# Windowed attention and a feed-forward layer: converting w_in further ahead, and giving a softmax's sums and divisions to GpSimd

## The chip, the cores and the metric

The kernel runs on one core of a Trainium2 chip, the other cores being unused. The metric is the device time of one execution in microseconds (us), the median of several runs. Engines are named as the profile names them: PE is TensorE (matmuls), DVE is VectorE, ACT is ScalarE, POOL is GpSimd, SP is SyncE, which here only issues transfers. PE and PEld are the two rows of TensorE, matmuls and weight loads.

## The reference

Eight heads of causal attention with a window of 128 positions and a linear bias, over 8 sequences of 576 positions, then a feed-forward layer (FFN) with a smooth rectifier:

```python
scores = scale * np.matmul(q, k.transpose(0, 1, 3, 2))          # q, k, v: (8, 8, 576, 64) float32
bias = slopes[:, None, None] * (-np.abs(rel).astype(np.float32))[None, :, :]
mask = (rel >= 0) & (rel < window)                              # window = 128
attn = softmax(np.where(mask, scores + bias[None], -1000000000.0))
x = np.matmul(attn, v)                                          # as (4608, 512)
h = x @ w_in                                                    # w_in: (512, 2048) float64
g = np.where(h >= 1, h, np.where(h <= -1, 0.0, (h + 1) ** 2 / 4))
return (g @ w_out).astype(np.float32)                           # w_out: (2048, 512) float64
```

The weights arrive in 64-bit floating point. The kernel has to turn them into 32-bit numbers itself, and it splits most of its operands into a high and a low 16-bit half, so that three 16-bit matmuls stand for one of higher precision.

## The kernel before, in words

**Tiling.** The 4608 rows are worked off in 12 chunks of 384 rows (three tiles of 128). For each chunk the attention of 8 heads is done as 4 pairs of heads, p = 4c to 4c + 3 for chunk c, and then the FFN over 16 blocks fc of 128 of the 2048 inner columns. While PE does the FFN of chunk c, the attention of chunk c + 1 is worked off between its blocks.

**Attention.** `scores` (L433) multiplies q and k of a pair. `soften` (L465) adds the bias and finds the maximum on DVE (L482, writes `z` and `nmax`), takes the exponential and its sum on ACT (L484), then on DVE sums up (L490), takes the reciprocal (L491), adds the two halves of z, which belong to neighbouring key blocks (L494), and multiplies by the reciprocal into `ep` (L495). `weights_t` (L499) transposes `ep` on PE (L504), copies on ACT (L508) and cuts out the two triangles on POOL (L509, L511) into `lu`. `values` (L525) multiplies by v on PE (L538), and `split_x` (L576) makes the 16-bit halves of x (L583, L584). `reach_of` and `reach_of_v` (L308, L380) take the largest value of v's rows on DVE (L385), for a common scale of x. `done_t[m]` marks the end of head m's `weights_t`.

**FFN.** `layer1` (L587) does 12 matmuls per block (L590 to L592) and the rectifier: `u` on ACT (L597), `g` in two steps on DVE (L598, L599). `done_g[fc]` marks the rectifier's instructions. `layer2` (L610) follows two blocks later; in chunk 0 it multiplies 32-bit numbers (L619), later 16-bit halves (L622 to L624), for which `g` is split by ACT and POOL (L606, L607).

**Weights.** In chunk 0's FFN the weights of each block are also brought in and converted. `fetch_weights(fc)` (L171) loads a block's w_in and w_out, 512 KB each, into one of three buffers `raw`, by two DMAs on ACT's queue (L173, L175). `convert_in` (L189) unfolds the two words on ACT (L180, L181), joins them on DVE (L185) and takes the largest value of each row (L194). `convert_out` (L216) joins w_out's words (L185) and scans them on ACT (L219). `scale_in` (L197) spreads the largest values over the partitions with a small PE matmul (`across`, L152, writes `m_i`) and works out the scale on DVE (L159 to L163). `split_in` (L204) makes the halves `wi` on ACT (L210) and DVE (L211). The first three blocks are converted during chunk 0's attention, each half of the work behind the head that `EARLY` (L761) names; `then` (L773) puts the scales and splits of blocks 0 and 1 and chunk 0's row reductions behind heads. In the FFN `convert_after(f)` (L749) converts block f + 3 and scales block f + 2 behind the rectifier of block f, and block f + 2 is split at the end of it.

**Order.** The program text gives each instruction a rank. A planner simulates the engines with costs of its own before the kernel is built and puts onto each engine, and into each DMA queue, the instruction of the best rank that is ready in its simulation. On the chip each engine and each queue then works strictly in that order. `behind(instructions, f)` (L238) forces what f issues behind the given instructions on the same engine. The attention's steps are a list, `segments` (L655 to L712), emitted as far as a count (`emit_attention`, L713); `ready[c]` marks the place in it from which chunk c's FFN can begin, and the loop at L799 emits a share of the next chunk's segments after each half block. Of pair 4, which is chunk 1's first, the scores stand ahead of the last values of chunk 0, so they come before chunk 0's FFN. `keep_busy` (L85) fills PE with transposes that nobody reads during chunk 0's attention.

Of the kernel before, what the change touches and what calls it, by code (L numbers as in the profile page):

```python
# [20 lines left out]
def windowed_attention_then_ffn(  # L21
# [26 lines left out]
    P = 128  # L48
# [92 lines left out]
    def column(name, tag, bufs=2, n=1):  # L141
        return ap1.tile([P, n], F32, name=name, tag=tag, bufs=bufs)
# [28 lines left out]
    def fetch_weights(fc):  # L171
        w = raw[fc] = rawp.tile([P, 2, DM, 2], I32, name=f"raw{fc}", tag=f"raw{fc % 3}")
        S.dma_start(w[:, 0].rearrange("p (c f) w -> p c f w", c=NCC),  # L173
                    wi32[:, 2 * fc * P:2 * (fc + 1) * P].rearrange("(c p) (f w) -> p c f w", p=P, w=2))
        S.dma_start(w[:, 1], wo32[fc * P:(fc + 1) * P, :].rearrange("p (f w) -> p f w", w=2))  # L175
# [11 lines left out]
    wide = {}  # L187

    def convert_in(fc):  # L189
        f = wide[fc] = wp.tile([P, DM], F32, name=f"f_i{fc}", tag="f_i", bufs=3)  # L190
        unfold(fc)
        float32_of(fc, 0, f)
        rows = column(f"rows_i{fc}", "rows")
        V.tensor_reduce(rows, f, X, ALU.max, apply_absolute_value=True)  # L194
        spread(f"i{fc}", rows)

    def scale_in(fc):  # L197
        s1, i1 = s_in[:, fc:fc + 1], i_in[:, fc:fc + 1]
        scale_of(f"i{fc}", s1, i1)
# [265 lines left out]
    def soften(m, blks, pt):  # L465
# [20 lines left out]
        if blks[-1] == NQB - 1:  # L486
            if c % CYCLE == 1:
                G.memset(z[:, 2, :D], 0.0)
            rc = st["rc"] = ap1.tile([P, 8], F32, name=f"rc_{m}", tag="rc", bufs=2)
            V.tensor_reduce(rc[:, :NQB], sm, mybir.AxisListType.X, ALU.add)  # L490
            V.reciprocal(rc[:, :NQB], rc[:, :NQB])  # L491

            n0 = 1 - b0
            f = V.tensor_tensor(z[:, n0:, P:], z[:, n0:, :P], z[:, n0:, P:], ALU.add)  # L494
            V.tensor_tensor(ep, z[:, :, P:], rc[:, :NQB].rearrange("p (i o) -> p i o", o=1).broadcast_to([P, NQB, P]), ALU.mult)  # L495
            st["held"] = f
# [158 lines left out]
    for p in range(p8):  # L655
        segments += [[lambda p=p: scores(p, (0, 1))], [lambda p=p: scores(p, (2,))]]
# [6 lines left out]
        if 2 <= p <= NPAIR:  # L663
            segments.append([lambda p=p: values(p - 2)])
        if 1 <= p <= NPAIR:
            turn(2 * p - 2)
            turn(2 * p - 1)
        if p >= NPAIR:
            segments.append([lambda p=p: values(p - 1)])
            if p == NPAIR:  # L670
                ready.append(len(segments))
            turn(2 * p)
            turn(2 * p + 1)
        d = 2 * p - (1 if p < NPAIR else 0)
        if p:
            segments += [[lambda d=d, x=x: behind(done_t[d], lambda: load_v(x, True))] for x in {1: (4, 5), 2: (6,), 3: (7,)}.get(p, ())]
            segments += [[lambda d=d, x=x: behind(done_t[d], lambda: load_all(x, True))] for x in {5: (8, 9), 6: (10,), 7: (11,)}.get(p, ())]
            segments += [[lambda d=d, x=x: behind(done_t[d], lambda: reach_of(x))] for x in {3: (4, 5), 4: (6, 7), 6: (8,), 7: (9,)}.get(p, ())]
# [41 lines left out]
    for i in range(NCHUNK * NFC + LAG):  # L720
# [24 lines left out]
        if c == 0 and fc + 2 < NFC:  # L745
            ops.append(lambda fc=fc: behind(done_g[fc], lambda: split_in(fc + 2)))
        ffn.append(ops)

    def convert_after(f):  # L749

        fc = f + LEAD
        if fc < NFC:
            if fc + 2 < NFC:
                behind(done_g[f], lambda: fetch_weights(fc + 2))
            behind(done_g[f], lambda: convert_in(fc))
            behind(done_g[f - 1 if f else f], lambda: convert_out(fc))
        if f + 2 < NFC:
            behind(done_g[f], lambda: scale_in(f + 2))


    EARLY = (2, 3, 4, 5, 7, 8)  # L761
# [17 lines left out]
    load_first(1)  # L779
    load_v(0)  # L780
# [6 lines left out]
    landed = S.copy(loaded, pair[0]["qr"][:, :1])  # L787
    behind([landed.ins], lambda: fetch_weights(0))
# [49 lines left out]
```

## Time and profile before

| what | value |
|---|---|
| median of 3 runs | 992.11 us (989.86 to 993.59) |
| the profiled execution's own time | 991.8 us |
| its span, first to last instruction | 989.7 us |
| mean granted PE clock | 0.989 |
| busy in the span: PE, DVE, ACT, POOL | 955.0, 731.6, 607.2, 340.6 us |
| bytes moved by DMA | 59.86 MB, mean 60 GB/s |

An instruction in the profile has an engine, a line of the kernel, an operation, the tile that it writes and those that it reads, and a start and a duration in us from the span's start. In square brackets stands how long its engine idled before it, and who ended that wait. A line of a group ends with the busy time, the mean duration in ns and the idle time ahead. A granted clock of 1.00 is TensorE's full speed. The first 44 us are chunk 0's attention, and up to about 155 us run the FFN of chunk 0 and the attention of chunk 1.

### The profile page before, as it was taken

To read this page: it belongs to the slowest core of one execution; us is meant where nothing else is said; L and a number is where in the kernel's file an instruction comes from. 1 tells how busy PE (TensorE), PEld (TensorE's weight loads), DVE (VectorE), ACT (ScalarE), POOL (GpSimd) and SP (SyncE) were. 2 spreads that over 40 slices of the span, in tenths; PEclk is the share of its full clock that TensorE was granted. 3 is DMA by queue.
4 is the path that set the end of the run, shared out by engine and by line. 5 is a ranking of instruction groups with operands and counts; after the bars stand their busy time and mean duration, and the time that the engine had idled before them with its cause. 6 is when DMAs were issued, how large, how long until landed. Compare 5 with 4: busy or idle time off the path is not lost.

```text
span 989.7 us, 17764 instructions
## 1 busy us (share of the span) xinstructions
PE 955.0 (96%) x6181; PEld 522.2 (53%) x6181; DVE 731.6 (74%) x2089; ACT 607.2 (61%) x1509; POOL 340.6 (34%) x446
## 2 busy tenths in 40 slices
PE   8798899998999999999999999999999999999997
PEld 5444344554555555555555555555555555555553
DVE  6899798896787787687787788677677886765332
ACT  6788777666656666565665665666666655644322
POOL 5311003333334432532533533433443443334221
PEclk9799999998999999999999999999999999999999
DMA  8476441012021011112111101111201000000000
GB/s 274 134 245 201 154 141 39 12 49 72 30 59 58 25 41 63 38 30 60 62 33 52 58 25 54 63 30 50 72 30 30 33 1 1 33 2 1 33 1 32
DMA packets 53290, 59.86 MB, mean 60 GB/s; under 512 B 3408, under 2 KB 42576, under 8 KB 53200
## 3 DMA queue, kind: packets, MB, share of 16 engines
q1 hardware_dynamic: 42304, 41.82, 13.7%
q10 hardware_dynamic: 10896, 16.91, 4.9%
q8 instruction: 48, 0.79, 0.3%
q14 instruction: 42, 0.34, 0.1%
HBM read 49.28 MB, written 9.44 MB: 59 GB/s over the span
## 4 chain that ended last, share of the span: by engine, by line
PE 85%; DVE 7%; ACT 4%; DMA 1%; issue 1%; POOL 1%; ACTq 0%; SPq 0%; POOLq 0%; DVEq 0%
PE h L590 12%; PE h L592 12%; PE h L591 12%; PE acc L622 12%; PE acc L623 12%; PE acc L624 12%; PE s L459 5%; PE x L561 4%; PE p L504 3%; ACT z L484 1%; PE acc L619 1%; DMA vn<-in_v_dram 1%; DVE g L598 1%; ACT raw L181 1%; DVE g L599 1%
## 5 line engine op out<-in xcount | busy, mean ns | idle before, releaser
L607 POOL TENSOR_TENSOR gl<-g,gh 128x384 f16<-128x384 f32 x176 | 167.2, 950 | 453.5 <-ACT gh L606 442.7
L598 DVE SCALAR_TENSOR_TENSOR g<-u,half 128x384 f32<-128x384 f32 x176 | 123.9, 705 | 157.1 <-ACT u L597 144.1
L606 ACT CAST gh<-g 128x384 f16<-128x384 f32 x176 | 89.6, 509 | 189.2 <-DVE g L599 102.1
L622 PE MATMUL acc<-wo,gh 128*128 128x512 f16 x528 | 200.3, 379 | 0.0
L623 PE MATMUL acc<-wo,gh 128*128 128x512 f16 x528 | 200.2, 379 | 0.0
L624 PE MATMUL acc<-wo,gl 128*128 128x512 f16 x528 | 196.0, 379 | 0.0
L597 ACT ACTIVATE u<-h,shift,fall 128x384 f32<-128x384 f32 x176 | 116.4, 663 | 98.9 <-PE h L592 98.9
L484 ACT ACTIVATE z<-z,nmax 128x256 f32<-128x256 f32 (+2 forms) x288 | 137.7, 480 | 33.1 <-DVE nmax L482 31.1
L590 PE MATMUL h<-x,wi 128*128 128x384 f16 x384 | 125.8, 329 | 4.6 <-ACT x L570 2.8
L590 PE MATMUL h<-xh,wi 128*128 128x384 f16 x384 | 125.2, 327 | 4.3 <-ACT wi L210 2.9
L592 PE MATMUL h<-xh,wi 128*128 128x384 f16 x384 | 125.3, 326 | 1.1 <-DVE wi L211 1.1
L592 PE MATMUL h<-x,wi 128*128 128x384 f16 x384 | 126.1, 328 | 0.0
L591 PE MATMUL h<-x,wi 128*128 128x384 f16 x384 | 126.0, 328 | 0.0
L591 PE MATMUL h<-xl,wi 128*128 128x384 f16 x384 | 125.4, 327 | 0.0
L482 DVE CUSTOM_DVE_ANT_0 z<-s,near,z_of 128x256 f32<-128x256 f32 (+2 forms) x240 | 98.6, 459 | 33.7 <-PE s L459 33.5
L599 DVE SCALAR_TENSOR_TENSOR g<-h,gain,g 128x384 f32<-128x384 f32 x176 | 108.1, 615 | 3.9
L590 PEld LDWEIGHTS <-wi 128*128 128x128 f16 x768 | 75.2, 98 | 67.1 <-issue 7.5
L591 PEld LDWEIGHTS <-wi 128*128 128x128 f16 x768 | 75.4, 98 | 59.1 <-issue 7.2
L592 PEld LDWEIGHTS <-wi 128*128 128x128 f16 x768 | 75.3, 98 | 53.9 <-issue 3.6
L519 POOL TENSOR_SCALAR_AFFINE_SELECT lu<-lu 128x768 f16<-128x768 f16 x80 | 70.4, 894 | 58.2 <-DVE lu L517 57.7
L624 PEld LDWEIGHTS <-gl 128*128 128x128 f16 x528 | 51.5, 98 | 59.0 <-issue 0.4
L622 PEld LDWEIGHTS <-gh 128*128 128x128 f16 x528 | 51.6, 98 | 51.0 <-issue 1.1
(148 smaller groups left out, 1445.7 us busy)
## 6 DMA issues: line engine op xcount, KB each, us to landing
out_dram<-o SPq DMA_DIRECT2D x35, 256.0 KB, 2.1
raw<-in_moe_w_in_dram ACTq DMA_DIRECT2D x16, 512.0 KB, 4.6
raw<-in_moe_w_out_dram ACTq DMA_DIRECT2D x16, 512.0 KB, 5.5
vn<-in_v_dram SPq DMA_DIRECT2D x32, 256.0 KB, 2.8
qk<-in_q_dram SPq DMA_DIRECT2D x40, 192.0 KB, 2.4
qk<-in_k_dram SPq DMA_DIRECT2D x28, 256.0 KB, 2.8
vn<-in_v_dram SPq DMA_DIRECT2D x16, 192.0 KB, 2.6
qk<-in_k_dram SPq DMA_DIRECT2D x12, 192.0 KB, 2.5
```

The source lines that it names most:

```text
L482: a = V.tensor_tensor_reduce(out=z[:, i, c0:], in0=pt[:, n, c0:], in1=r[:, c0:], op0=ALU.add, op1=ALU.min, scale=factor, scalar=3.0e38, ac ...
L484: b = S.activation(z[:, i, c0:], z[:, i, c0:], AF.Exp, bias=nmax[:, i:i + 1], scale=-1.0, accum_out=sm[:, i, 0:1])
L590: T.matmul(ph, wi[fc][:, 0, cc, :], xh, start=(cc == 0), stop=False)
L591: T.matmul(ph, wi[fc][:, 0, cc, :], xl, start=False, stop=False)
L592: T.matmul(ph, wi[fc][:, 1, cc, :], xh, start=False, stop=(cc == NCC - 1))
L597: first = S.activation(u, ph, AF.Relu, bias=shift[c] if c else quarter, scale=fall[c][:, col])
L598: V.scalar_tensor_tensor(g, u, half[c] if c else 0.5, u, ALU.min, ALU.mult)
L599: last = V.scalar_tensor_tensor(g, ph, gain[c][:, col] if c else fall[c][:, col], g, ALU.mult, ALU.max)
L607: G.tensor_tensor(gl, g, gh, ALU.subtract)
L622: T.matmul(a, gh[:, ts], wo[fc][:, 0], start=first, stop=False)
L623: T.matmul(a, gh[:, ts], wo[fc][:, 1], start=False, stop=False)
L624: T.matmul(a, gl[:, ts], wo[fc][:, 0], start=False, stop=last)
```

## The change

- **Conversion further ahead.** Up to block 5 of the FFN two tables (`CONVERT`, `SPLIT`) say which blocks are converted and split behind the rectifier of block f. Behind block 1 and block 3 two blocks are converted, behind 2 and 4 two are split. From then on block f + 5 is converted and block f + 4 scaled and split. The column `rows` of the largest values has four buffers for that instead of two. `EARLY` has the heads 6 and 7 instead of 7 and 8 for block 2.
- **Weight transfers** are issued from SP's queue instead of ACT's. In the FFN they are no longer forced behind the rectifier, so only their buffer holds them back. Those of block 0 are issued ahead of v and of the q and k of pairs 2 and 3, without the wait for the first q; for blocks 1 and 2 a single-element memset on POOL, behind the head named, holds the transfer back.
- **Softmax of chunk 1.** For the heads of chunk 1 the addition L494 and the multiplication L495 are done by POOL instead of DVE. For all chunks DVE's marker `held`, which is part of `done_t`, is the reciprocal instead of the addition.
- **Order.** The last values and transposes of chunk 0 stand ahead of pair 4's scores, and `ready[1]` with them. The row reductions of v of pairs 4 to 7 are all placed behind head 8; before, those of pairs 4 and 5 were behind head 5 and those of 6 and 7 behind head 8.

```diff
@@ fetch_weights
-        S.dma_start(w[:, 0]..., wi32[...])
-        S.dma_start(w[:, 1], wo32[fc * P:(fc + 1) * P, :].rearrange("p (f w) -> p f w", w=2))
+        if 0 < fc < 3:
+            G.memset(w[:1, :, 0, :1], 0)
+        DMA.dma_start(w[:, 0]..., wi32[...])
+        DMA.dma_start(w[:, 1], wo32[fc * P:(fc + 1) * P, :].rearrange("p (f w) -> p f w", w=2))
@@ convert_in
-        rows = column(f"rows_i{fc}", "rows")
+        rows = column(f"rows_i{fc}", "rows", 4)
@@ soften
-            V.reciprocal(rc[:, :NQB], rc[:, :NQB])
+            f = V.reciprocal(rc[:, :NQB], rc[:, :NQB])
             n0 = 1 - b0
-            f = V.tensor_tensor(z[:, n0:, P:], z[:, n0:, :P], z[:, n0:, P:], ALU.add)
-            V.tensor_tensor(ep, z[:, :, P:], rc[:, :NQB]...broadcast_to([P, NQB, P]), ALU.mult)
+            E = G if c == 1 else V
+            E.tensor_tensor(z[:, n0:, P:], z[:, n0:, :P], z[:, n0:, P:], ALU.add)
+            E.tensor_tensor(ep, z[:, :, P:], rc[:, :NQB]...broadcast_to([P, NQB, P]), ALU.mult)
             st["held"] = f
@@ the list of segments
     for p in range(p8):
+        if p == NPAIR:
+            segments.append([lambda p=p: values(p - 2)])
+            turn(2 * p - 2)
+            turn(2 * p - 1)
+            segments.append([lambda p=p: values(p - 1)])
+            ready.append(len(segments))
         segments += [[lambda p=p: scores(p, (0, 1))], [lambda p=p: scores(p, (2,))]]
...
-        if 2 <= p <= NPAIR:
+        if 2 <= p < NPAIR:
             segments.append([lambda p=p: values(p - 2)])
-        if 1 <= p <= NPAIR:
+        if 1 <= p < NPAIR:
...
         if p >= NPAIR:
-            segments.append([lambda p=p: values(p - 1)])
-            if p == NPAIR:
-                ready.append(len(segments))
+            if p > NPAIR:
+                segments.append([lambda p=p: values(p - 1)])
...
-  reach_of(x) for x in {3: (4, 5), 4: (6, 7), 6: (8,), 7: (9,)}.get(p, ())
+  reach_of(x) for x in {4: (4, 5, 6, 7), 6: (8,), 7: (9,)}.get(p, ())
@@ the FFN
-        if c == 0 and fc + 2 < NFC:
-            ops.append(lambda fc=fc: behind(done_g[fc], lambda: split_in(fc + 2)))
+        if c == 0:
+            ops.append(lambda fc=fc: split_after(fc))
@@ convert_after
-        fc = f + LEAD
-        if fc < NFC:
-            if fc + 2 < NFC:
-                behind(done_g[f], lambda: fetch_weights(fc + 2))
-            behind(done_g[f], lambda: convert_in(fc))
-            behind(done_g[f - 1 if f else f], lambda: convert_out(fc))
-        if f + 2 < NFC:
-            behind(done_g[f], lambda: scale_in(f + 2))
-    EARLY = (2, 3, 4, 5, 7, 8)
+        for fc in CONVERT.get(f, (f + 5,)):
+            if fc < NFC:
+                if fc + 2 < NFC:
+                    fetch_weights(fc + 2)
+                behind(done_g[f], lambda: convert_in(fc))
+                behind(done_g[f], lambda: convert_out(fc))
+        for fc in SPLIT.get(f, (f + 4,)):
+            if fc < NFC:
+                behind(done_g[f], lambda: scale_in(fc))
+    def split_after(f):
+        for fc in SPLIT.get(f, (f + 4,)):
+            if fc < NFC:
+                behind(done_g[f], lambda: split_in(fc))
+    CONVERT = {0: (3,), 1: (4, 5), 2: (6,), 3: (7, 8)}
+    SPLIT = {0: (2,), 1: (3,), 2: (4, 5), 3: (6,), 4: (7, 8)}
+    EARLY = (2, 3, 4, 5, 6, 7)
@@ the start
     load_first(1)
+    fetch_weights(0)
     load_v(0)
...
-    landed = S.copy(loaded, pair[0]["qr"][:, :1])
-    behind([landed.ins], lambda: fetch_weights(0))
```

More of the change, by code (lines that the diff above doesn't have):

```diff
@@ L172, in fetch_weights @@
         w = raw[fc] = rawp.tile([P, 2, DM, 2], I32, name=f"raw{fc}", tag=f"raw{fc % 3}")
-        S.dma_start(w[:, 0].rearrange("p (c f) w -> p c f w", c=NCC),
-                    wi32[:, 2 * fc * P:2 * (fc + 1) * P].rearrange("(c p) (f w) -> p c f w", p=P, w=2))
-        S.dma_start(w[:, 1], wo32[fc * P:(fc + 1) * P, :].rearrange("p (f w) -> p f w", w=2))
+        if 0 < fc < 3:
+            G.memset(w[:1, :, 0, :1], 0)
+        DMA.dma_start(w[:, 0].rearrange("p (c f) w -> p c f w", c=NCC),
+                      wi32[:, 2 * fc * P:2 * (fc + 1) * P].rearrange("(c p) (f w) -> p c f w", p=P, w=2))
+        DMA.dma_start(w[:, 1], wo32[fc * P:(fc + 1) * P, :].rearrange("p (f w) -> p f w", w=2))
     def unfold(fc, which=slice(0, 2)):
@@ L185, in float32_of @@
         V.scalar_tensor_tensor(out.bitcast(I32), raw[fc][:, a, :, 1], 3, raw[fc][:, a, :, 0], ALU.logical_shift_left, ALU.bitwise_or)
-    wide = {}
+    wide, rows_i = {}, {}
     def convert_in(fc):
@@ L490, in soften @@
             V.tensor_reduce(rc[:, :NQB], sm, mybir.AxisListType.X, ALU.add)
-            V.reciprocal(rc[:, :NQB], rc[:, :NQB])
+            f = V.reciprocal(rc[:, :NQB], rc[:, :NQB])
             n0 = 1 - b0
-            f = V.tensor_tensor(z[:, n0:, P:], z[:, n0:, :P], z[:, n0:, P:], ALU.add)
-            V.tensor_tensor(ep, z[:, :, P:], rc[:, :NQB].rearrange("p (i o) -> p i o", o=1).broadcast_to([P, NQB, P]), ALU.mult)
+            E = G if c == 1 else V
+            E.tensor_tensor(z[:, n0:, P:], z[:, n0:, :P], z[:, n0:, P:], ALU.add)
+            E.tensor_tensor(ep, z[:, :, P:], rc[:, :NQB].rearrange("p (i o) -> p i o", o=1).broadcast_to([P, NQB, P]), ALU.mult)
             st["held"] = f
@@ L677, in windowed_attention_then_ffn @@
             segments += [[lambda d=d, x=x: behind(done_t[d], lambda: load_all(x, True))] for x in {5: (8, 9), 6: (10,), 7: (11,)}.get(p, ())]
-            segments += [[lambda d=d, x=x: behind(done_t[d], lambda: reach_of(x))] for x in {3: (4, 5), 4: (6, 7), 6: (8,), 7: (9,)}.get(p, ())]
+            segments += [[lambda d=d, x=x: behind(done_t[d], lambda: reach_of(x))] for x in {4: (4, 5, 6, 7), 6: (8,), 7: (9,)}.get(p, ())]
     segments += [[lambda: behind(done_t[M1 - 2], lambda: reach_of(p8 + 2))],
```

## The prediction

> **What bounds the kernel now.** I read the page's head and its slices first, then the busy times by stretch. In the stretches the columns are the stretch, its length, the busy time of TensorE (PE), its weight loads, VectorE (DVE), ScalarE (ACT) and GpSimd (POOL), the granted clock, DMA share and rate.
>
> ```profile
> span 989.7 us, 17764 instructions
> PE 955.0 (96%) x6181; PEld 522.2 (53%) x6181; DVE 731.6 (74%) x2089; ACT 607.2 (61%) x1509; POOL 340.6 (34%) x446
> ...
> 20.00:44.00 24.00, 16.16 (x77) 8.87 (x78) 22.91 (x82) 20.09 (x51) 8.18 (x17) 0.79 0.61 194
> 44.00:160.00 116.00, 103.39 (x497) 52.31 (x496) 100.39 (x312) 92.76 (x193) 11.04 (x31) 0.99 0.50 167
> 160.00:228.00 68.00, 68.00 (x457) 37.23 (x455) 58.63 (x148) 43.65 (x107) 28.21 (x30) 1.00 0.09 26
> 228.00:242.00 14.00, 9.56 (x68) 5.34 (x67) 10.35 (x33) 10.79 (x29) 3.43 (x5) 0.76 0.32 108
> ```
>
> From 160 us on PE is full but for the hole at 228 to 242, and nothing in the change touches that part. What can be won lies before: 24.00 - 16.16 = 7.8 us of idle PE from 20 to 44 (end of chunk 0's attention, at a clock of 0.79) and 116.00 - 103.39 = 12.6 us from 44 to 160 (chunk 0's FFN with chunk 1's attention). In that second stretch DVE is busy 87% and ACT 80%: the three engines are close together, and POOL, at 11 us, is the only free one.
>
> What PE waited for from 40 to 160 (total us, times, longest), and the pitch of the blocks, from the rectifier's first step:
>
> ```profile
> PE acc L619 <- DVE g L599: 4.3, 4, 3.1
> PE h L590 <- ACT wi L210: 2.9, 4, 1.6
> PE m_i L152 <- DVE rows_i L194: 2.4, 4, 0.9
> PE h L592 <- DVE wi L211: 1.1, 2, 0.8
> ...
> L597 ACT ACTIVATE u<-h,quarter,fall x16: 648/665/688, 49.0 to 145.0; 128x384 f32<-128x384 f32 x16
> ```
>
> Split weights that came late cost 2.9 + 1.1 = 4.0 us, a late g 4.3. The pitch is (145.0 - 49.0) / 15 = 6.4 us a block.
>
> **The sum, against the profiled execution's own 991.8 us** (span 989.7); the median of the runs, 992.1, is 0.3 above it.
>
> *1. The row reductions of v leave the head.* reach_of for pairs 4 to 7 now stands behind head 8. Two of the four stood in DVE's queue ahead of the divisions of chunk 0's softmax:
>
> ```profile
> 22.50 0.69 DVE L385 TENSOR_REDUCE rows<-vn 128x1 f32<-128x512 f32 x1 [0.73 <-DMA vn<-in_v_dram]
> 23.34 0.69 DVE L385 TENSOR_REDUCE rows<-vn 128x1 f32<-128x512 f32 x1
> ...
> 24.00 0.55 DVE L495 TENSOR_TENSOR ep<-z,rc 128x384 f32<-128x384 f32 x1
> ...
> 24.70 0.52 PE L504 MATMUL p<-ident,ep 128*128 128x128 f32 x3 [2.51 <-DVE rc L491]
> ```
>
> DVE had nothing else from 22.50 - 0.73 to 24.00, and PE stood for 2.51 us. Bounds 0 (ACT, 84% busy here, comes last instead) and 2.5; nearest to the upper, I take **-2.0**. The reductions return later as 4 x 0.69 = 2.8 us of DVE.
>
> *2. Pair 4's scores go behind the first FFN block.* In the chain of waits they stand in the head; the same shapes later run at full clock:
>
> ```profile
> 29.93 2.94 PE s L443 x9
> 35.19 0.94 PE s L443 x2
> ...
> 68.06 1.13 PE L443 MATMUL s<-kr,ql 64*128 64x256 f32 x8
> 73.90 0.60 PE L443 MATMUL s<-kr,ql 64*128 64x192 f32 x4
> ...
> 32.90 0.43 DVE L482 CUSTOM_DVE_ANT_0 z<-s,rel 128x256 f32<-128x256 f32 x1
> 36.46 0.35 DVE L482 CUSTOM_DVE_ANT_0 z<-s,rel 128x192 f32<-128x192 f32 x1
> ```
>
> 3.9 us leave the chain and 1.73 come back: **-2.2**. Bounds 0 and the head's remaining idle, about 5. Their six score steps on DVE (first and last shown, together 6 x 0.4 = 2.4 us) move too.
>
> *3. w_in split four blocks back, converted five.* Before, block f+2 was split behind rectifier f and f+3 converted. The same instructions are issued, ahead of need, so the 4.0 us named above go: **-4.0**. Bounds 0 (the planner places by its own clock, and a queue position ahead of need isn't forced) and 5.2, with half of the 2.4 us for m_i, PE's own step of the same scales.
>
> *4. The late g.* One wait makes 3.1 of the 4.3 us, and it is dearer than it looks:
>
> ```profile
> 104.62 2.74 PE L619 MATMUL acc<-wf,g 128*128 128x512 f32 x6
> 110.48 4.17 PE L619 MATMUL acc<-wf,g 128*128 128x512 f32 x6 [3.07 <-DVE g L599]
> ...
> 112.00:115.00 3.00, 3.00 (x6) 1.07 (x5) 2.25 (x8) 0.72 (x1) 0.00 (x0) 0.50 0.00 0
> ```
>
> After 3.07 idle us the six matmuls took 4.17 for 2.74, at a granted clock of 0.50: another 1.4. Of 4.3 + 1.4 = 5.7, between 0 and all, I take half, since DVE is no emptier than before (next): **-2.9**.
>
> *5. POOL does the sums and divisions of chunk 1.* Sixteen operations leave DVE. POOL's nearest two-input row is gl; below it lies the one-input select. Then the DVE operations with two operands in SBUF, and what one met while gl ran:
>
> ```profile
> L495 DVE TENSOR_TENSOR ep<-z,rc 128x384 f32<-128x384 f32 x8 | 4.9, 639 | 0.0
> L494 DVE TENSOR_TENSOR z<-z 128x384 f32<-128x384 f32 x8 | 4.4, 549 | 0.0
> L607 POOL TENSOR_TENSOR gl<-g,gh 128x384 f16<-128x384 f32 x176 | 167.2, 950 | 453.5 <-ACT gh L606 442.7 <-PE x L561 4.1 <-PE acc L624 2.9
> L511 POOL TENSOR_SCALAR_AFFINE_SELECT lu<-lu 128x384 f32<-128x384 f32 x8 | 4.8, 603 | 0.4
> L211 DVE SCALAR_TENSOR_TENSOR wi<-f_i,s_in,wi 128x512 f16<-128x512 f32 x15 | 11.5, 765 | 1.7 <-ACT wi L210 1.7
> L185 DVE SCALAR_TENSOR_TENSOR wf<-raw 128x512 int32<-128x512 int32 x14 | 10.2, 730 | 0.0
> L185 DVE SCALAR_TENSOR_TENSOR f_i<-raw 128x512 int32<-128x512 int32 x13 | 8.9, 688 | 2.2 <-ACT raw L181 2.2
> L598 DVE SCALAR_TENSOR_TENSOR g<-u 128x384 f32<-128x384 f32 x16 | 8.8, 551 | 6.9 <-ACT u L597 6.7
> ...
> 159.99 1.06 POOL L607 TENSOR_TENSOR gl<-g,gh 128x384 f16<-128x384 f32 x1 [0.60 <-ACT gh L606]
> 160.20 1.26 DVE L598 SCALAR_TENSOR_TENSOR g<-u,half 128x384 f32<-128x384 f32 x1
> ```
>
> DVE loses 4.9 + 4.4 = 9.3 us. POOL gains 16 x 0.95 = 15.2 (16 x 0.60 = 9.6 at least), which its 105 free us hold. But L598, 0.55 alone, took 1.26 beside gl: 0.7 more. There are 15 + 14 + 13 + 16 = 58 such DVE operations, of 0.68 us on average; with 16 POOL operations in about 110 us, 58 x 16 x (0.95 + 0.68) / 110 = 14 of them meet one, at half of 0.7: 5 us. DVE's account of the stage is 100.4 - 9.3 + 2.8 + 2.4 + 5 = 101.3: not relieved at all. So I book no gain here, and a cost, since the two heads' ep now come 4 x 0.95 instead of 2 x (0.549 + 0.639) = 2.4 us after the exponentials, 1.4 us later in each of four pairs; PE mostly has layer matmuls to do meanwhile. Bounds 0 and the slow rival's 16.8; near the lower, as wi is no longer late: **+2.0**.
>
> The Trainium skill speaks against this edit (SBUF — State Buffer, "Who interferes with whom"): a VectorE instruction with two SBUF inputs and a GpSimd instruction that reads SBUF exclude each other, and the later one blocks fully. The row of L598 agrees in kind; by the rule a met operation would wait out half of a POOL operation on average, about 0.48 instead of 0.35 us, which makes 14 x 0.48 = 6.7 instead of 5 us of DVE, an estimate from that page and the rows, and 987.2 for the forecast if PE felt all of the difference.
>
> *6. Doubled blocks.* Behind rectifiers 1 and 3 two blocks are converted, behind 2 and 4 two are split. ACT, for one:
>
> ```profile
> L180 ACT ACTIVATE raw<-raw 128x1024 f32<-128x1024 f32 x13 | 14.9, 1147 | 1.1 <-issue 1.1
> L181 ACT ACTIVATE raw<-raw 128x1024 int32<-128x1024 uint32 x13 | 14.7, 1132 | 0.0
> L219 ACT ACTIVATE junk<-wf 128x512 bf16<-128x512 f32 x13 | 8.1, 622 | 2.9 <-DVE s_in L163 1.6 <-DVE top_i L161 1.3
> ```
>
> An extra conversion is 1.15 + 1.13 + 0.62 = 2.9 us of ACT, twice 5.8; with 20% of ACT idle, 2.6 of the 12.8 us of two blocks cover part. Bounds 0 and 5.8: **+2.0**.
>
> *7. Weight DMAs on SP's queue.* ACT waited 1.1 us for its own issues (row L180); that is off PE's path: 0. The first block's weights now stand ahead of v and of pairs 2 and 3 in SP's order. They were in flight beside them already, so the bytes ahead of pair 2's k are nearly the same: **+0.5**, bounds 0 and 2. The memsets that hold blocks 1 and 2 back are single elements; DVE's marker for "softmax done" moves from the sum to the reciprocal, a step earlier: 0 both.
>
> Sum: 991.8 - (2.0 + 2.2 + 4.0 + 2.9) + (2.0 + 2.0 + 0.5) = 991.8 - 11.1 + 4.5 = 985.2; with the 0.3 to the median **985.5**. Its own range is 981.5 to 989.
>
> **Rivals.** *More:* with wi two blocks ahead PE never waits in the stage: 12.6 + 2.0 + 2.2 = 16.8 us go, 975.3 with the 0.3. For it: the named waits have few sources. Against: DVE's 101.3 us would have to fit into 116 - 12.6 = 103.4, 98% busy. Its range is 975 to 981.5.
>
> *No change:* the doubled blocks cost PE their whole 5.8, and one wait with its 1.4 of slow clock follows: 985.5 - 2.0 + 5.8 + 1.4 = 990.7. Also here: the planner leaves the order much as it was, items 1 and 2 alone, 992.1 - 4.2 = 987.9. For it: ACT and DVE have little room, and the work only moves forward. Against: by the rows ACT and DVE still idle 23 and 15 us in the stage, and two blocks of lead let that idle time be used.
>
> *A fetch stuck on SP.* SP's queue before:
>
> ```profile
> SPq L304 <- POOL vn L376: 34.9, 3, 14.3
> ```
>
> A fetch queued behind a load that waits 14.3 us lands late by that less two blocks' lead (12.8), plus the landing itself, some 6: 985.5 + 7.5 = 993. It decides if it happens once. The ACT queue was free of it.
>
> *Slower:* ep late on POOL. The transposes stand in PE's queue in order; if POOL's four operations take 0.95 + 0.35 each, 5.2 for 2.4, PE stands 2.8 us in each of four pairs, and loses 1.4 more to the slow clock: 4 x 4.2 = 16.8. 985.5 - 2.0 + 16.8 = 1000.3. It turns the sign from 8.6 / 4 = 2.2 us a pair. For it: L598's 1.26. Against: with wi ahead, PE has a block's layer matmuls to do at each such place (the six of layer 2 alone are 2.74 us).
>
> **Chances.** A measurement tells about 0.5%, 5 us. Forecast 0.45 (0.41 of it faster, under 987.1), more 0.13, no change 0.22, stuck fetch 0.06, slower 0.14 (0.13 beyond 997.1). Faster 0.41 + 0.13 = 0.54; slower 0.13 plus 0.02 of the no-change case's tail = 0.15; within 0.31. The range leaves out the far half of "more" and of "slower": 976.5 to 997.5.
>
> **What would show it.** Item 1: no wait of over 1 us at the transposes near 24 us. Item 2: the first rectifier near 44 to 45 us instead of 49.05. Item 3: no wait of PE on wi after block 2. Item 4: no half-clock stretch between 60 and 150. Item 5: L598 above 0.6 us, POOL some 15 us fuller, DVE's busy time in the stage within 3 us of 100. Item 6: PE waits between rectifiers 1 and 5. I am wrong if DVE is clearly relieved, if PE waits for ep by microseconds, or if the hole at 228 us changes by more than 4 us, which I left as it is.

## The result, and the profile after

The changed kernel takes 983.78 us (median of 4 runs, 983.55 to 984.24), beside 992.45 us (989.86 to 993.59) for the kernel before, measured here with one run more than above. The ratio is 0.9912, with a 95% interval of 0.9892 to 0.9932: about 8.7 us faster. In the new kernel most line numbers stand two or three higher (the rectifier's steps at L600 to L602, layer 1 at L593 to L595, `ep` at L498, the transposes at L507).

The page's head of the changed kernel, then its busy times by stretch (same columns as before):

```profile
span 981.8 us, 17793 instructions
...
PE 954.0 (97%) x6181; PEld 523.0 (53%) x6181; DVE 722.9 (74%) x2073; ACT 607.3 (62%) x1508; POOL 357.6 (36%) x464
```

```profile
20.00:44.00 24.00, 17.73 (x98) 9.54 (x96) 20.54 (x69) 20.33 (x50) 7.89 (x17) 0.86 0.67 226
44.00:160.00 116.00, 108.62 (x522) 55.93 (x520) 101.26 (x316) 95.60 (x201) 31.09 (x50) 0.99 0.49 162
...
60.00:150.00 90.00, 86.51 (x423) 44.83 (x423) 78.74 (x259) 74.27 (x160) 21.85 (x37) 1.00 0.52 171
```

PE is fuller in both stretches that the change touches: 17.73 for 16.16 us in the head, 108.62 for 103.39 from 44 to 160. The half-speed stretch at 112 us is gone (clock 1.00 from 60 to 150), but a new one stands at 49.6 to 53.0 us (clock 0.50), shortly behind a wait of PE for pair 4's ep. Over the whole span DVE has 8.7 us less to do (722.9 for 731.6) and POOL 17.0 more (357.6 for 340.6).

Where the time came from is read from two groups, the rectifier's first step and chunk 0's layer 2 (columns: fewest, median and most ns of one, then first and last start), first of the kernel before, whose row of the rectifier is in the prediction, then of the changed one:

```profile
L619 PE MATMUL acc<-wf,g x96: 592/592/1057, 51.0 to 154.8; 128*128 128x512 f32 x96
```

```profile
L600 ACT ACTIVATE u<-h,quarter,fall x16: 648/656/678, 45.5 to 138.6; 128x384 f32<-128x384 f32 x16
L622 PE MATMUL acc<-wf,g x96: 592/592/1222, 50.0 to 146.8; 128*128 128x512 f32 x96
```

The first rectifier starts 49.0 - 45.5 = 3.5 us earlier. The 15 blocks up to the last one take 93.1 instead of 96.0 us, 2.9 less. From there to the last matmul of chunk 0's layer 2 it is 8.2 instead of 9.8, 1.6 less. Together 8.0, and the span is 7.9 shorter: in this profile everything was won before 155 us.

One execution isn't like another in the head. The changed kernel was profiled once more (the last run under "The queue and the doubled blocks"):

```profile
L600 ACT ACTIVATE u<-h,quarter,fall x16: 648/667/680, 47.2 to 139.9; 128x384 f32<-128x384 f32 x16
```

Here the first rectifier is only 1.8 us earlier than before, the last matmul of chunk 0's layer 2 starts at 148.2, 6.6 earlier, and the span is 982.5, 7.2 shorter. So the gain at the stage's end shows in both profiles, but how much of it lies in the head is known to 1.7 us only.

Nor is the gain even over the blocks. The fifth rectifier, before and changed:

```profile
74.65 0.65 ACT L597 ACTIVATE u<-h,quarter,fall 128x384 f32<-128x384 f32 x1
```

```profile
75.55 0.66 ACT L600 ACTIVATE u<-h,quarter,fall 128x384 f32<-128x384 f32 x1
```

From the first rectifier to the fifth it takes 30.1 instead of 25.6 us (30.0 in the second profile), so the whole head start is used up there. The eleven blocks behind it take 63.0 instead of 70.4.

What PE waited for from 40 to 160 in the changed kernel (total us, times, longest), complete:

```profile
PE p L507 <- POOL ep L498: 2.9, 2, 2.7
PE acc L622 <- DVE g L602: 1.6, 3, 0.9
PE m_i L152 <- DVE rows_i L196: 1.2, 2, 0.8
PE h L593 <- DVE g L602: 1.1, 1, 1.1
PE h L593 <- DVE r L406: 0.5, 1, 0.5
```

The waits for wi are gone, those of layer 2 for g fell from 4.3 to 1.6 us, and a wait for ep, now from POOL, came in.

### The profile page after: what moved, and what is told of

It reads as the page before. It is cut to its first block, busy times and chain, and to the rows that moved or that the text cites. A ratio compares the mean times of both kernels' runs of the same rounds, so it can differ in the third digit from the quotient of the medians.

```text
span 981.8 us, 17793 instructions
## 1 busy us (share of the span) xinstructions
PE 954.0 (97%) x6181; PEld 523.0 (53%) x6181; DVE 722.9 (74%) x2073; ACT 607.3 (62%) x1508; POOL 357.6 (36%) x464
## 4 chain that ended last, share of the span: by engine, by line
PE 89%; DVE 4%; ACT 4%; DMA 1%; issue 1%; SPq 0%; POOL 0%; ACTq 0%; DVEq 0%; POOLq 0%
PE h L593 13%; PE h L595 12%; PE h L594 12%; PE acc L625 12%; PE acc L626 12%; PE acc L627 12%; PE s L461 5%; PE x L564 4%; PE p L507 3%; PE acc L622 3%; PE x L541 1%; ACT z L486 1%; ACT raw L183 1%; PE s L445 1%; DMA k<-in_k_dram 1%
## 5 line engine op out<-in xcount | busy, mean ns | idle before, releaser
L601 DVE SCALAR_TENSOR_TENSOR g<-u,half 128x384 f32<-128x384 f32 x176 | 121.9, 693 | 156.8 <-ACT u L600 146.4
L600 ACT ACTIVATE u<-h,shift,fall 128x384 f32<-128x384 f32 x176 | 116.6, 665 | 99.8 <-PE h L595 99.6
L593 PE MATMUL h<-x,wi 128*128 128x384 f16 x384 | 125.7, 329 | 3.1 <-DVE g L602 1.5
L593 PE MATMUL h<-xh,wi 128*128 128x384 f16 x384 | 124.8, 327 | 2.5 <-DVE g L602 2.5
L595 PE MATMUL h<-x,wi 128*128 128x384 f16 x384 | 125.9, 328 | 0.0
L595 PE MATMUL h<-xh,wi 128*128 128x384 f16 x384 | 125.0, 326 | 0.0
L602 DVE SCALAR_TENSOR_TENSOR g<-h,gain,g 128x384 f32<-128x384 f32 x176 | 108.2, 615 | 3.9
L593 PEld LDWEIGHTS <-wi 128*128 128x128 f16 x768 | 75.1, 98 | 63.1 <-issue 7.1
L595 PEld LDWEIGHTS <-wi 128*128 128x128 f16 x768 | 75.2, 98 | 52.3 <-issue 4.0
L627 PEld LDWEIGHTS <-gl 128*128 128x128 f16 x528 | 51.5, 98 | 58.7 <-issue 0.4
```

The source lines that it names most:

```text
L593: T.matmul(ph, wi[fc][:, 0, cc, :], xh, start=(cc == 0), stop=False)
L595: T.matmul(ph, wi[fc][:, 1, cc, :], xh, start=False, stop=(cc == NCC - 1))
L600: first = S.activation(u, ph, AF.Relu, bias=shift[c] if c else quarter, scale=fall[c][:, col])
L601: V.scalar_tensor_tensor(g, u, half[c] if c else 0.5, u, ALU.min, ALU.mult)
L602: last = V.scalar_tensor_tensor(g, ph, gain[c][:, col] if c else fall[c][:, col], g, ALU.mult, ALU.max)
L627: T.matmul(a, gl[:, ts], wo[fc][:, 0], start=False, stop=last)
```

## The experiments

The theory was the sum's: lead −4.9 (items 3, 4 and 6), order −4.2 (items 1 and 2), POOL +2.0 (item 5), queue +0.5 (item 7), each independent of the others. The rivals were that one part makes the whole gain, and that the parts depend on each other. Differences in us below are ratios times 992.5; an interval of ±0.002 is ±2 us, a difference of two ratios is uncertain by some 2.5 to 3 us, and by the medians some differences come out up to 2 us otherwise. The runs are told by argument and not in the order in which they were made: the four that take a part out of the change came first.

### The lead alone

The kernel before with `CONVERT`, `SPLIT`, `split_after`, the four buffers of `rows`, and `convert_out` behind the rectifier of block f instead of f - 1; transfers stay on ACT's queue, forced behind the rectifier.

```diff
-        fc = f + LEAD
+        for fc in CONVERT.get(f, (f + 5,)):
...
-        if f + 2 < NFC:
-            behind(done_g[f], lambda: scale_in(f + 2))
+        for fc in SPLIT.get(f, (f + 4,)):
+            if fc < NFC:
+                behind(done_g[f], lambda: scale_in(fc))
```

> The kernel before (992.4 us) with the two tables alone: w_in converted five and split four blocks ahead; the transfers stay on ACT's queue behind the rectifier, the order of the head and the softmax stay. My sum: 4.0 for wi and 2.9 for g less 2.0 for doubled blocks, 4.9 us, 987.5, with no wait of PE for wi after block 2. The rival, since the changed kernel with the old lead showed no wait for wi either: the lead as such removes nothing, 991 to 993, and PE's waits move to another tile.

Measured: 986.7 us, ratio 0.9943 [0.9925, 0.9960], 5.7 us faster. Of its waits of PE those of layer 2 for g and those for wi, and its rectifiers:

```profile
PE acc L619 <- DVE g L599: 1.9, 3, 0.9
...
PE h L590 <- ACT wi L210: 0.8, 1, 0.8
...
PE h L592 <- DVE wi L211: 0.3, 1, 0.3
```

```profile
L597 ACT ACTIVATE u<-h,quarter,fall x16: 647/668/682, 48.7 to 137.5; 128x384 f32<-128x384 f32 x16
```

The head is as before (48.7), the blocks take 88.8 instead of 96.0 us. The waits for wi went from 4.0 to 1.1 (both that are left stand at about 61 us, ahead of block 2's rectifier) and those for g from 4.3 to 1.9, as items 3 and 4 said. This gain isn't even either. The fifth rectifier starts at 78.20, 29.5 us behind the first instead of 25.6, and the eleven blocks behind it take 59.3 instead of 70.4 us: the blocks with the doubled work take 3.9 us more, and the later ones 11.1 less.

### The order alone

The kernel before with chunk 0's last values and transposes ahead of pair 4's scores, `reach_of` behind head 8, and the new `EARLY`.

```diff
+        if p == NPAIR:
+            segments.append([lambda p=p: values(p - 2)])
+            turn(2 * p - 2)
+            turn(2 * p - 1)
+            segments.append([lambda p=p: values(p - 1)])
+            ready.append(len(segments))
...
-  reach_of(x) for x in {3: (4, 5), 4: (6, 7), 6: (8,), 7: (9,)}
+  reach_of(x) for x in {4: (4, 5, 6, 7), 6: (8,), 7: (9,)}
```

> The kernel before with the order of the head alone (pair 4's scores behind chunk 0's last values, row reductions of pairs 4 to 7 behind head 8, block 2 behind heads 6 and 7). My sum: 4.2 us less, 988.2, the first rectifier near 45.5 us. The rival, that the stage after it is bound by DVE and gives the start back: 991 to 993 with the first rectifier early all the same.

Measured: 996.41 us, ratio 1.0047 [1.0031, 1.0063], 4.7 us slower. Its rectifiers, its waits of PE from 40 to 160, a stretch, and DVE's timeline (start, us, instruction):

```profile
L597 ACT ACTIVATE u<-h,quarter,fall x16: 647/662/671, 42.9 to 146.1; 128x384 f32<-128x384 f32 x16
```

```profile
PE acc L619 <- DVE g L599: 7.7, 6, 2.3
PE h L592 <- DVE rows L388: 2.3, 1, 2.3
PE h L590 <- ACT wi L210: 2.0, 1, 2.0
```

```profile
43.00:150.00 107.00, 92.48 (x411) 46.73 (x411) 88.26 (x280) 79.15 (x159) 11.79 (x30) 0.94 0.53 172
```

```profile
47.82 2.45 DVE L385 TENSOR_REDUCE rows<-vn 128x1 f32<-128x512 f32 x4
...
50.78 0.55 DVE L598 SCALAR_TENSOR_TENSOR g<-u 128x384 f32<-128x384 f32 x1
```

The first rectifier comes 6.1 us earlier, more than items 1 and 2 said, and the blocks then take 103.2 instead of 96.0 us: all of it is given back and more. The four moved reductions stand in one piece ahead of the second block's g. PE waits for g, and 2.3 us at a matmul for which the profile names L388; that matmul reads wi, whose DVE half (L211) ended 0.06 us before it began, so it is rather the split behind the reductions that was late. The mean granted clock is 0.94 here, beside 0.98 over the same stretch of the kernel before. At the end of chunk 0's layer 2 the kernel is only 0.6 us behind (155.4 for 154.8): an earlier start of the FFN is worth nothing where the engines that feed it are not free. The other 4.1 of the 4.7 us that the profile is longer come later ("The parts together").

### The softmax on POOL alone

The kernel before with this edit only:

```diff
-            V.reciprocal(rc[:, :NQB], rc[:, :NQB])
+            f = V.reciprocal(rc[:, :NQB], rc[:, :NQB])
...
-            f = V.tensor_tensor(z[:, n0:, P:], z[:, n0:, :P], z[:, n0:, P:], ALU.add)
-            V.tensor_tensor(ep, ...)
+            E = G if c == 1 else V
+            E.tensor_tensor(z[:, n0:, P:], z[:, n0:, :P], z[:, n0:, P:], ALU.add)
+            E.tensor_tensor(ep, ...)
```

> The kernel before (992.4 us) with GpSimd's part of the change alone: chunk 1's additions and multiplications on GpSimd, and the marker of a softmax's end at the reciprocal. My sum: 2.0 us slower than before, 994.4, with PE waiting for ep. The rival, DVE relieved: the late g (4.3 us and 1.4 of slow clock) goes and it takes 987 to 990.

Measured: 996.16 us, ratio 1.0045 [1.0027, 1.0063], 4.5 us slower. PE's wait for ep from 40 to 160, its rectifiers, and POOL's timeline at the end of the head (`ep` is pair 4's, `lu` the triangles of chunk 0's last heads):

```profile
PE p L505 <- POOL ep L496: 5.5, 4, 3.7
```

```profile
L598 ACT ACTIVATE u<-h,quarter,fall x16: 651/670/679, 51.5 to 152.8; 128x384 f32<-128x384 f32 x16
```

```profile
40.65 0.83 POOL L496 TENSOR_TENSOR ep<-z,rc 128x384 f32<-128x384 f32 x1
41.43 0.52 POOL L512 TENSOR_SCALAR_AFFINE_SELECT lu<-lu 128x384 f32<-128x384 f32 x1
41.92 1.26 POOL L496 TENSOR_TENSOR ep<-z,rc 128x384 f32<-128x384 f32 x1
43.14 0.97 POOL L512 TENSOR_SCALAR_AFFINE_SELECT lu<-lu 128x384 f32<-128x384 f32 x1
```

and POOL's last select of chunk 0 in the kernel before:

```profile
41.08 0.52 POOL L511 TENSOR_SCALAR_AFFINE_SELECT lu<-lu 128x384 f32<-128x384 f32 x1
```

With the old order, pair 4 is softened while chunk 0's last triangles are being cut. On one in-order engine the last select ends at 44.1 instead of 41.6, and the first rectifier starts at 51.5 instead of 49.0, 2.5 late in both. That this is the place is borne out by leaving pair 4 on DVE, all else as in this kernel:

```diff
-            E = G if c == 1 else V
+            E = G if c == 1 and p > NPAIR else V
```

> The kernel before (992.4 us) with GpSimd's part alone, and there for pairs 5 to 7 only; with pair 4 too it took 996.2. My theory, that pair 4's operations stood in GpSimd's queue between the selects of chunk 0's last heads: the first rectifier is back near 49 us from 51.5, and 2.5 to 4 us of the loss are gone, 992 to 994. The rival, that the operations' length and the shared port make the loss wherever they stand: still 995 to 997.

Measured: 992.06 us (12 runs, 987.66 to 993.91), ratio 0.9980 [0.9964, 0.9997], and the first rectifier is back at 49.0:

```profile
L598 ACT ACTIVATE u<-h,quarter,fall x16: 647/670/682, 49.0 to 145.8; 128x384 f32<-128x384 f32 x16
```

So pair 4 on POOL costs 6.5 us by the ratios (4.5 by the medians) where it stands between the selects, 2.5 of them before the first rectifier. The rival, that the operations cost this wherever they stand, expected 995 to 997. The blocks too take longer in the first kernel (101.3 against 96.8 us); which of its edits' consequences does that was not singled out. The profiled run of the second is the fastest of its twelve, so the 96.8 flatters it.

### The change without the lead, without the order

> The changed kernel with w_in converted three and split two blocks ahead, as before, in every block; order, transfers on SP's queue and GpSimd's part as changed. My sum: the 4.0 us of waits for wi return, the 2.0 for doubled blocks go, and half of the late g (2.9) may return: 983.8 + 2.0 to 4.9, so 986 to 989, with PE waits for wi of 3 us or more in the profile. The rival, that the order of the head makes nearly all of the gain, expects 983 to 985 and hardly a wait for wi.

The changed kernel with both tables at the old distances:

```diff
-    CONVERT = {0: (3,), 1: (4, 5), 2: (6,), 3: (7, 8)}
-    SPLIT = {0: (2,), 1: (3,), 2: (4, 5), 3: (6,), 4: (7, 8)}
+    CONVERT = {f: (f + 3,) for f in range(NFC)}
+    SPLIT = {f: (f + 2,) for f in range(NFC)}
```

Measured: 988.28 us, ratio 0.9968 [0.9955, 0.9981], 5.6 us dearer than the whole change. But the place isn't where item 3 has it. Chunk 0's layer 2 in this kernel, and 20 us about the end of chunk 1's FFN, then the same place of the changed kernel:

```profile
L622 PE MATMUL acc<-wf,g x96: 592/592/1061, 51.4 to 148.2; 128*128 128x512 f32 x96
```

```profile
221.00:241.00 20.00, 13.07 (x94) 7.93 (x93) 16.22 (x48) 12.84 (x36) 6.34 (x8) 0.83 0.31 93
```

```profile
218.00:238.00 20.00, 15.92 (x107) 9.45 (x105) 14.76 (x49) 13.61 (x37) 8.48 (x10) 0.74 0.28 95
```

Among its waits of PE from 40 to 160 there is none for wi (the longest is 1.9 us, for ep), and chunk 0's FFN ends only 148.2 - 146.8 = 1.4 us later than in the first profile of the changed kernel. Of the 4.4 us in the span, 3.0 come behind it, most of it in the hole where chunk 2's FFN waits for its x: PE idles 6.93 instead of 4.08 us there. Beside the second profile of the changed kernel, whose layer 2 ends at 148.2 too, all of the 3.7 us come behind it. What the lead has to do with that hole isn't settled.

> The changed kernel with the order of the head as before: pair 4's scores ahead of chunk 0's last values, the row reductions of pairs 4 to 7 behind heads 5 and 8, block 2 converted behind heads 7 and 8. My sum: items 1 and 2 return, 2.0 + 2.2 us, 988.0, and the first rectifier is back near 49 us instead of 45.5. The rival, that the first FFN block's start doesn't matter because DVE and ACT set the stage's end, expects 983 to 985.

The changed kernel with the old list of segments, the old `reach_of` and `EARLY` (the reverse of the second diff above): 988.36 us, ratio 0.9962 [0.9949, 0.9975], 5.0 us dearer than the whole. The first rectifier is as late as with the softmax alone (in POOL's timeline pair 4's operations stand between the selects again):

```profile
L600 ACT ACTIVATE u<-h,quarter,fall x16: 648/667/729, 52.3 to 141.4; 128x384 f32<-128x384 f32 x16
```

### The change with the softmax back on DVE

```diff
-            E = G if c == 1 else V
+            E = V
```

> The changed kernel (983.8 us) with chunk 1's additions and multiplications back on DVE, all else kept. By my sum GpSimd's share of the change cost 2.0 us, so this takes 981.8, the one wait of PE for GpSimd's ep near 48 us (2.7 us, with slow clock after it) is gone, and DVE's busy time in the stretch from 44 to 160 us stays within 3 us of 101. The rival, that taking 9.3 us off DVE is what gives the conversions their room, expects it slower: 983.8 plus up to 9.3 less 5 of contention, 988, with PE waiting for g or for rows_i again.

Measured: 985.36 us, ratio 0.9943 [0.9923, 0.9963]: 3.1 us dearer than the change by the ratios, 1.6 by the medians. A place where the two differ is pair 4's softmax. DVE and PE in this kernel, then POOL and PE in the changed one:

```profile
46.50 0.55 DVE L497 TENSOR_TENSOR z<-z 128x384 f32<-128x384 f32 x1
...
48.00 2.43 DVE L387 TENSOR_REDUCE rows<-vn 128x1 f32<-128x512 f32 x4
50.35 0.55 DVE L601 SCALAR_TENSOR_TENSOR g<-u 128x384 f32<-128x384 f32 x1
...
50.90 0.52 DVE L498 TENSOR_TENSOR ep<-z,rc 128x384 f32<-128x384 f32 x1
...
51.48 0.55 PE L507 MATMUL p<-ident,ep 128*128 128x128 f32 x3 [4.06 <-DVE ep L498]
```

```profile
44.79 1.95 POOL L497 TENSOR_TENSOR z<-z 128x384 f32<-128x384 f32 x2 [7.15 <-ACT z L486]
46.83 1.61 POOL L498 TENSOR_TENSOR ep<-z,rc 128x384 f32<-128x384 f32 x2
...
47.70 0.55 PE L507 MATMUL p<-ident,ep 128*128 128x128 f32 x3 [2.70 <-POOL ep L498]
```

In the new order the four reductions stand on DVE between the sums and the ep of pair 4. On POOL, ep passes them: from the first addition to the transposes it is 47.70 - 44.79 = 2.9 us instead of 51.48 - 46.50 = 5.0, and PE waits 2.70 instead of 4.06 us. The second profile of the changed kernel, whose first addition starts as late as in this kernel (46.36 us), has the transposes at 49.31, 2.2 us earlier than here, after a wait of 1.88. Putting back pair 4 alone (`c == 1 and p > NPAIR`, as above) says the same:

> The changed kernel (983.8 us) with pair 4's additions and multiplications on DVE, those of pairs 5 to 7 on GpSimd as changed. My theory now, that GpSimd's share is harmful where pair 4 meets the end of chunk 0 and useful later: the wait of PE for ep near 48 us (2.7 us, and some 1.5 of slow clock) goes, 980 to 982. The rival, that DVE is the later one there (with all of it on DVE PE waited 4.1 us for ep at that place): 984 to 986.

Measured: 986.12 us, ratio 0.9934 [0.9918, 0.9951], beside 984.09 for the changed kernel, taken once more on the same chip (expectation below). Neither of the two differences is far outside its uncertainty, but both point the same way. Between these two kernels, that is for pairs 5 to 7 on POOL, only 0.9 us are left, which can't be told from none: as far as these runs tell, the gain is pair 4's.

What POOL's work costs DVE is read from the operations with two operands in SBUF, first with the softmax on DVE, then in the changed kernel (count, then total busy us and mean ns):

```profile
L213 DVE SCALAR_TENSOR_TENSOR wi<-f_i,s_in,wi 128x512 f16<-128x512 f32 x16 | 12.3, 782 | 2.2 <-ACT wi L212 2.2
L187 DVE SCALAR_TENSOR_TENSOR wf<-raw 128x512 int32<-128x512 int32 x16 | 12.0, 748 | 1.0 <-ACT raw L183 1.0
L187 DVE SCALAR_TENSOR_TENSOR f_i<-raw 128x512 int32<-128x512 int32 x16 | 11.2, 700 | 0.3 <-ACT raw L183 0.3
L601 DVE SCALAR_TENSOR_TENSOR g<-u 128x384 f32<-128x384 f32 x16 | 8.8, 548 | 1.0 <-ACT u L600 1.0
```

```profile
L187 DVE SCALAR_TENSOR_TENSOR wf<-raw 128x512 int32<-128x512 int32 x16 | 12.6, 785 | 2.1 <-ACT raw L183 2.1
L213 DVE SCALAR_TENSOR_TENSOR wi<-f_i,s_in,wi 128x512 f16<-128x512 f32 x16 | 12.2, 767 | 2.7 <-ACT wi L212 2.7
L187 DVE SCALAR_TENSOR_TENSOR f_i<-raw 128x512 int32<-128x512 int32 x16 | 11.5, 719 | 0.5 <-ACT raw L183 0.5
L601 DVE SCALAR_TENSOR_TENSOR g<-u 128x384 f32<-128x384 f32 x16 | 9.4, 590 | 3.5 <-ACT u L600 3.5
```

The four groups sum to 44.3 and 45.7 us (45.8 in the second profile): with POOL at work DVE takes 1.4 us more in them, not 5. One meeting can be seen in the changed kernel: a join into wf that starts at 65.31 us, beside POOL's additions from 65.26 on, takes 1.49 us, where the group has a mean of 0.75 with the softmax on DVE.

### The queue and the doubled blocks

> The kernel before with the weight transfers alone moved: on SP's queue, held back only by their buffer, block 0's ahead of v, memsets for blocks 1 and 2. My sum: 0.5 us slower, 992.9, with the waits for wi as before (some 4 us). The rival, that the free transfers are what ended the waits for wi in the changed kernel with the old lead: 988 to 990 and under 1 us of waits for wi.

The kernel before with the weight transfers on SP's queue, block 0's ahead of v, unforced, and the memsets: 991.4 us, ratio 0.9989 [0.9977, 1.0001]. PE's waits for wi are 2.4 + 0.7 us, so the free transfers alone don't end them, as the rival expected them to. The edit in the FFN:

```diff
...
-                behind(done_g[f], lambda: fetch_weights(fc + 2))
+                fetch_weights(fc + 2)
...
```

> The changed kernel (983.8 us) with the weight transfers back on ACT's queue, behind the first q and behind the rectifiers, all else as changed. My sum: 0.5 us faster, 983.3. The rival, that the transfers' new place carries part of the gain: 985 to 988, with ACT waiting for raw or PE for wi.

The reverse, the changed kernel with them back on ACT's queue: 984.09 us, ratio 0.9925 [0.9909, 0.9941], against 0.9912. Neither shows a cost or a gain that can be told from none.

> The changed kernel with a lead of four blocks for the conversion and three for the split, so that only one block has two conversions and one has two splits. My sum's item 6: one of the two doublings' 2.0 us goes, and the third block of lead is not needed: 982.8. The rival, that every block of lead is room for the attention's bursts: 985 to 988, with more waits of PE for g and for rows_i.

The changed kernel with one doubled block and a lead of four and three blocks instead of two doubled ones and five and four:

```diff
-        for fc in CONVERT.get(f, (f + 5,)):
+        for fc in CONVERT.get(f, (f + 4,)):
...
-        for fc in SPLIT.get(f, (f + 4,)):
+        for fc in SPLIT.get(f, (f + 3,)):
...
-    CONVERT = {0: (3,), 1: (4, 5), 2: (6,), 3: (7, 8)}
-    SPLIT = {0: (2,), 1: (3,), 2: (4, 5), 3: (6,), 4: (7, 8)}
+    CONVERT = {0: (3,), 1: (4, 5)}
+    SPLIT = {0: (2,), 1: (3,), 2: (4, 5)}
```

> The changed kernel once more, on the same chip as these: 983.8 us by every theory. It is the reference for the three others.

Measured on one chip: 984.51 us, ratio 0.9916 [0.9900, 0.9931], and for the unaltered change 984.09 us, ratio 0.9912 [0.9896, 0.9928]. What the second doubling and the fifth block of lead cost or bring can't be told from nothing. PE waits longer for g without them (2.6 + 2.2 us instead of 1.6 + 1.1), as the rival had it, but the time isn't its 985 to 988.

### The parts together

The ratios in one table; those marked * have the transfers on SP's queue too, which by its two runs is worth about a microsecond.

| | old order | new order |
|---|---|---|
| neither | 1 | 1.0047 |
| lead | 0.9943 | 0.9943* |
| softmax on POOL | 1.0045 | 0.9968* |
| both | 0.9962* | 0.9912* |

The new order costs 4.7 us on its own, nothing with the lead, and gains 7.6 with the softmax on POOL and 5.0 with both. The softmax on POOL costs 4.5 us on its own and 1.9 with the lead, and gains 7.8 on the new order, 3.1 with both. Only the lead gains beside each of them: 5.7 alone, 8.2 and 10.3 beside one of the others, 5.6 with both. By the uncertainty named above the 1.9 isn't told from none and the 3.1 barely. The part effects alone sum to −5.7 + 4.7 + 4.5 − 1.1 = +2.4 us; together they make −8.7. The rival that the parts depend on each other is the one that holds. For order and softmax the traces show why: the new order takes pair 4 on POOL away from chunk 0's selects, and on POOL pair 4's ep passes the reductions that the new order moved. Since the planner places the whole kernel anew for each edit, every difference here holds some of its placement as well; how much wasn't measured.

Where the time lies is another matter. From each kernel's profile, the start of the last matmul of chunk 0's layer 2, and what is left of the span from there:

| kernel | layer 2's last matmul at, us | span left, us |
|---|---|---|
| before | 154.8 | 834.9 |
| lead alone | 149.7 | 835.3 |
| order alone | 155.4 | 839.0 |
| softmax on POOL alone | 162.0 | 832.5 |
| change without the lead | 148.2 | 838.0 |
| change without the order | 153.9 | 832.7 |
| change without the softmax on POOL | 149.2 | 834.6 |
| changed, two profiles | 146.8, 148.2 | 835.0, 834.3 |

The right column differs by up to 6.5 us, although no part of the change works there. In the profiles of this table PE is busy all the time from 165 to 215 us and for the same share from 250 us to 970, so nearly all of the difference arises at the hole between, where chunk 2's FFN waits for its x. That is where most of the loss of the order alone lies, and all that the lead is worth within the change if the second profile is taken, while the lead alone gains in the stage itself. No run shows what sets the length of the hole, and each row is one profile.

## Why the prediction came near

The forecast was 985.5 us, 6.6 faster than before; measured are 983.78, 8.7 faster, inside its own range. The head's part of the sum, items 1, 2 and 7, was −3.7 at the first rectifier. It came 3.5 earlier in one profile of the changed kernel, 1.8 in the other, and 6.1 with the order alone, so that the 3.5 stands so near is luck at least in part. The stage's part, −4.0 − 2.9 + 2.0 + 2.0 = −2.9, measured −4.5 and −4.8. That the sum came so near owes something to errors that cancelled: it added the items as if each had its price everywhere, and the tables show that they don't.

- **Item 1** is right in place, and its test holds: the transposes near 24 us waited 0.16 us (at 22.66). But PE waited again just behind them, in the changed kernel:

```profile
24.57 1.30 PE L541 MATMUL x<-lu,vn 128*64 128x256 f32 x10 [1.36 <-POOL vn L378]
```

  The wait of 2.51 us became 0.16 + 1.36, the larger part on another cause: about 1.0 us went, where 2.0 was booked. The upper bound was too near: the next releaser came soon behind.
- **Items 1 and 2 together** failed as a term that stands alone. The step that failed is "The reductions return later as 4 x 0.69 = 2.8 us of DVE": it booked them as busy time of the stage, and in the order alone they stand ahead of the second block's g and eat up the early start. With the lead alone beside it the order is worth nothing; with lead and POOL the term is worth 5.0 us, near the 4.2 booked.
- **Item 3** is right for the lead alone: the waits for wi fell by 2.9 us there, and it is worth 5.7 us beside 4.9 for items 3, 4 and 6. In the whole change no such wait is left, but the run without the lead has none either, and its loss of 5.6 us lies for the most part behind the stage (3.0 of 4.4 us by one profile of the changed kernel, all of 3.7 by the other), where the prediction has no term. So order and POOL together do away with the named waits too, and what the lead gives beside them isn't explained.
- **Item 4** is right: no slow clock from 60 to 150, and the waits of layer 2 for g fell by 2.7 us; with the 1.4 us of slow clock at 112 us, which is gone, 4.1 where 2.9 was taken. The new slow stretch at 50 us belongs to item 5's place.
- **Item 5** has the wrong sign. It took +2.0, and within the change the softmax on POOL gains 1.6 to 3.1 us. Two steps failed. The contention of 5 us was 1.4 (58 operations, 14 meetings and 0.35 us each was an estimate from one pair of rows, a long gl beside one g, and that g was of chunk 1, whose operation takes 0.62 by the median and not 0.55). By the rule of the Trainium skill (SBUF — State Buffer, "Who interferes with whom") the estimate was 6.7 and is further off; the extra time agrees with the rule in kind only, and corresponds to some 3 meetings of 0.48 us instead of 14. And ep was taken to come 1.4 us later than on DVE, by durations alone; what stands ahead of it in DVE's queue, the moved reductions with 2.43 us, was left out. The DVE total of the stage did come out (101.26 us, 101.3 forecast), but not for the reason given: the stretch holds 5.2 us more of PE's work, and over the span DVE was relieved by 8.7 of the 9.3 us (by 6.4 beside the kernel with the softmax back on DVE, 729.3). That was named as a sign of being wrong, and here it was. So was a wait of PE for ep by microseconds, and it came as well: 2.70 us at pair 4, and the six matmuls of layer 2 shortly behind it took 4.31 us instead of 2.74. On DVE the same place is no better (4.06 us, then 4.30).
- **Item 6** took +2.0. Taking out one of the two doublings changed nothing that can be told, but the cost does show where the item put its sign, between rectifiers 1 and 5: with the lead alone they take 3.9 us more, in the changed kernel 4.5 (30.1 for 25.6), and there 5.3 of PE's 7.3 us of waits lie between 44 and 75 us, 2.9 of them for pair 4's ep. It is work brought forward, and the later blocks return more than that. Over the stage ACT and DVE had the room: they idle 116 - 95.60 = 20.4 and 14.7 us in it even now.
- **Item 7** is right: one wait of 0.67 us of scores for k in the head, where 0.5 was booked (row below; the second profile has none), a first rectifier 0.4 us later with the transfers alone (49.4), and no effect that the ratios can tell.

```profile
11.45 0.67 PE L445 MATMUL s<-k,qr 64*128 64x256 f32 x2 [0.67 <-DMA k<-in_k_dram]
```

Better sizes of the terms don't mend the sum: with 1.0 for item 1, 4.1 for item 4 and a gain of 1.6 for item 5 it would be 985.5 + 1.0 - 1.2 - 3.6 = 981.7, 2.1 off instead of 1.7. What one part wins another would have won too, as the waits for wi show.

Of the rivals, the slow one, ep late on POOL, has its mechanism in the softmax alone (PE waits 5.5 us for ep there, and the first rectifier comes 2.5 late), but at 4.5 us and not the 16.8 of its price, and the place is POOL's queue between the selects: with pairs 5 to 7 alone on POOL there is no loss. The new order removes that meeting. The rival "more" didn't come: PE still idles 116 - 108.62 = 7.4 us from 44 to 160. A fetch stuck for 14 us didn't show (of SP's waits with the weight fetches the longest is 6.3 us), nor did the doubled blocks' 5.8 us in the whole time. The hole behind chunk 1's FFN moved with the rest and changed little, as assumed: PE is busy 15.92 us at a clock of 0.74 of the 20 shown above, and in the kernel before 15.56 at 0.83:

```profile
224.00:244.00 20.00, 15.56 (x110) 8.63 (x108) 12.64 (x40) 12.85 (x33) 8.12 (x10) 0.83 0.24 79
```

## What to carry to other kernels

Before adding up the parts of a change, ask of each which other part makes room for it. An earlier start is worth its microseconds only if nothing holds up the stage behind it: here the order lost 4.7 us alone, gained nothing beside the lead, and gained 5.0 to 7.6 us where the softmax had gone to POOL, so that pair 4's ep could pass the reductions that the order had moved. A move to a free engine pays only if nothing urgent of another chain stands in that engine's queue at that moment. A slower engine can still deliver sooner than a fast one with a queue; compare what stands ahead of the operation on each, not the durations alone. Test a part both alone and by taking it out of the whole: here two parts that lose by themselves gain in company. And look in the trace for where a difference arises before putting it down to the part: several of these arose behind the stage that was changed.

## What was not expected of the hardware

Most of POOL's additions and multiplications took nearly the same time, and the longest of each half as long again. The tile's view of the changed kernel (fewest, median and most ns):

```profile
L497 POOL TENSOR_TENSOR z<-z x8: 995/1002/1456, 44.8 to 116.9; 128x384 f32<-128x384 f32 x8
L498 POOL TENSOR_TENSOR ep<-z,rc x8: 821/826/1275, 46.8 to 118.8; 128x384 f32<-128x384 f32 x8
```

The medians lie within 7 ns of the fewest, and the longest take 0.45 us more. By these medians POOL's multiplication is a sixth faster than its addition, while on DVE before both take 548 ns by the median (the mean of 639 in the prediction's row holds one of 1272). By the sums of DVE's four groups above, the sixteen POOL operations cost DVE 1.4 us in all, 0.09 each.
